# Row-tiled K and Q projections in one visit, MoE weights loaded ahead of batch 1, and a new planner, in a fused attention and MoE kernel

## The chip, the cores and the metric

The kernel runs on one core of one Trainium2 chip. The metric is the time of one execution on the device in microseconds (us), given as the median of several executions. The kernel before takes 329.5 us (329.06 to 330.17 in four runs).

Five engines work side by side (busy in the kernel before: TensorE 95% of the span, ScalarE 60%, VectorE 58%, GpSimd 26%), each through its own list of instructions in the order that the program fixes: TensorE (PE in the profile; its weight loads are PEld), VectorE (DVE), ScalarE (ACT), GpSimd (POOL) and SyncE (SP). POOL and SP also issue the transfers (DMA), 42 and 167 of them in the profile of the kernel before. An engine waits on a semaphore when the program does not yet allow its next instruction; TensorE did not go past such a wait here: in the changed kernel it stood 4.1 us before one instruction while later work was ready (shown below).

## The reference

```python
# q, k, v: 8 batches x 8 heads x 576 rows x 64; omega: 128 features x 64
def phi(x):                                        # random-feature map
    proj = np.einsum('bhsd,md->bhsm', x, omega)
    h = proj - np.sum(x * x, axis=-1, keepdims=True) / 2.0
    h = h - np.max(h, axis=-1, keepdims=True)
    return np.exp(h) / np.sqrt(m)
q_p, k_p = phi(q * scale), phi(k * scale)
kv, z = einsum('bhsm,bhsd->bhmd', k_p, v), np.sum(k_p, axis=2)
attn = einsum('bhsm,bhmd->bhsd', q_p, kv) / (einsum('bhsm,bhm->bhs', q_p, z)[..., None] + 1e-6)
x = attn.transpose(0, 2, 1, 3).reshape(4608, 512)  # tokens x features
h = x @ w_in                                       # 512 x 2048
out = (h / (1 + np.exp(-1.702 * h))) @ w_out       # 2048 x 512
```

A batch has 576 rows a head: 512 "main" rows and 64 "last" rows. The kernel works on pairs of heads, four pairs a batch.

## The kernel before

A small planner in Python builds a graph of operations, each with an engine, an assumed cost, a key (its priority) and its reads and writes. It then plays the program through with its assumed costs and so fixes the order of instructions on every engine; semaphores keep that order right whatever the real times are. A load has a `gate`, the transfer that must have landed before it is issued.

The projections of one pair (cut). `T` holds the transposed main rows, even head in partitions 0 to 63 and odd head in 64 to 127; `omB` is omega twice with zeros, so that a 128-row matmul picks one head:

```python
for hd, t0, c0, o in (("a", 2, 0, 1280), ("b", 6, 4, 1792)):       # K: 4 matmuls of 256 columns
    gr = bank()
    g.add(PE, [mm(at(gr, 0, 256), Tb(t0), omB[:, :]), mm(at(gr, 256, 512), Tb(t0 + 1), omB[:, :])],
          240, key, reads=[("Tk", tt)] + OM, grp=gr)
    reduce(0, 4, c0, gr); exp(gr, 512, o, ["k" + hd], key + 200)
gr = bank()                                                        # last rows: 2 of 128
g.add(PE, [mm(at(gr, 128, 256), TLo, om_o), mm(at(gr, 0, 128), om_e, TLo)], 115, key + K_L, ...)
...
for nm, w_, o in (("q0", om_e, 0), ("q1", om_o, 512)):             # Q: 2 of 512
    gr = bank()
    g.add(PE, mm(at(gr, 0, 512), w_, Tq), 216, key + K_Q, ...); exp(gr, 512, o, [nm], ...)
```

After these, a weights exp (WW), V times weights on POOL (VP), KV on TensorE, its copy (KVZ), the output matmuls, a division (RD, OO), and a transpose into XT, on TensorE for batches 0 and 1 and by DMA from batch 2 on. XT feeds the MoE in nine blocks of 512 tokens, one for the main rows of each batch and one for all last rows: for each block 16 groups of four 128x512 matmuls with WIN, tanh on ACT, a product on DVE (GT), then 64 matmuls with WOUT.

The loads of batches 0 and 1 and the weights. `load_qk` and the weights go through POOL's queue, `load_ql` (the last rows of Q and K, QLF) and `load_v` through SP's:

```python
load_qk(0, 0, 2, -150, "p0");  load_ql(0, ...);  load_v(0, 0, 2, -149)
load_qk(0, 2, 2, -148, "p1");  load_qk(0, 4, 4, -147, "p2")
load_v(0, 2, 2, -147, after=[("k", 0, 0)])
load_qk(1, 0, 4, P["LD"] + -10, "a", after=[("k", 0, 0)])     # batch 1's first half, early
gate = [("q", 0, 1)]                                          # Q of batch 0's second pair
load_ql(1, -119, P["ql1"], after=gate);  load_v(1, 0, 2, -110, after=gate)
gate = [("q", 0, 2)]
for c in range(4): load_win(c, P["LD"] + -5 + c, after=gate)
load_qk(1, 4, 4, P["LD"] + 0, "b", after=gate)
load_v(1, 2, 2, -109, after=[("win", 2)])
for c in range(4): load_wout(c, P["LD"] + 10 + c, after=gate)
```

The gate `("q", 0, 1)` is the Q load of batch 0's second pair. In the expectations quoted below I call it "the third Q load" by a slip; the edits name it as meant.

The softmax here doesn't subtract the row's maximum and nothing guards it: scores larger than these inputs give would overflow.

## Time and profile before

| what | value | seen in |
|---|---|---|
| span of the profiled run | 328.3 us | page |
| TensorE busy | 311.3 us, 95% | busy table |
| MoE: 1,152 matmuls of 512 columns, 216 ns apart | 249 us | timeline |
| K and Q of a pair, batch 2 on: 4 x 109 + 2 x 216 ns | 868 ns | timeline |
| last rows of four pairs: 8 x 56 ns | 448 ns | timeline |
| first matmul / first MoE matmul | 4.27 / 29.9 us | timeline |
| end of the last matmul | 324.3 us | timeline |

The page's busy table and slices of the kernel before (each slice is 8.2 us; a digit is the busy share in tenths; PEclk is the granted TensorE clock):

```profile
PE 311.3 (95%) x2091; PEld 163.2 (50%) x2129; DVE 189.5 (58%) x420; ACT 197.1 (60%) x396; POOL 86.6 (26%) x176
...
PE   2697999999999999999999999999999999999995
...
PEclk9989999999999999999999999999999999999999
DMA  7999989989999999969979973311121011000033
```

TensorE is full from the fifth slice to the last but one. DMA is at 90% or more in 18 of the 40 slices, all in the first 190 us, and yet TensorE's waits after 56 us are next to nothing (the profile lists none of them).

The timeline of TensorE before, at a pair of a late batch (start us, duration us, instruction):

```profile
182.92 0.38 PE L363 MATMUL PB<-TT,omB 128*128 128x512 bf16 x1
183.13 0.38 PE L363 MATMUL PB<-omB,TT 128*128 128x256 bf16 x2
183.35 1.03 PE L363 MATMUL OB<-WOUT,GT 128*128 128x512 bf16 x4
...
186.25 0.38 PE L363 MATMUL PB<-omB,TT 128*128 128x256 bf16 x2
186.47 0.22 PE L363 MATMUL PB<-omB,TL 128*128 128x128 bf16 x1
186.53 0.22 PE L363 MATMUL PB<-TL,omB 128*128 128x128 bf16 x1
186.58 0.59 PE L363 MATMUL OB<-WOUT,GT 128*128 128x512 bf16 x2
```

Read the starts, not the durations: Q's 512 columns take 183.13 - 182.92 = 0.21 us, two of K take 0.22, and a pair's last rows take 0.11.

### The profile page before, as it was taken

The numbers are of one execution on the slowest core, as the hardware profiler recorded it, in microseconds if no ns is written. First come the engines' busy times: TensorE is split into PE (matmuls) and PEld (weight loads), VectorE is DVE, ScalarE is ACT, GpSimd is POOL, SyncE is SP. The second block draws the span as 40 slices with busy tenths as digits, with TensorE's granted clock in tenths as the row PEclk, the third lists the DMA queues.
The fourth block names the chain that finished last, engine by engine and source line by source line (L and its number), as shares of the span: only waits on it lengthen the run. The fifth ranks groups of instructions, "written<-read, shape, count | busy, mean of one in ns | idle before, by whom it ended". The sixth has DMA issues, their size and how long they took to land.

```text
span 328.3 us, 5569 instructions
## 1 busy us (share of the span) xinstructions
PE 311.3 (95%) x2091; PEld 163.2 (50%) x2129; DVE 189.5 (58%) x420; ACT 197.1 (60%) x396; POOL 86.6 (26%) x176
## 2 busy tenths in 40 slices
PE   2697999999999999999999999999999999999995
PEld 1474655455555555555555555555544444444442
DVE  3397975458538786677468667675565434434300
ACT  2879664567738868777566657665663434344411
POOL 8398043043425226233316022222220000000000
PEclk9989999999999999999999999999999999999999
DMA  7999989989999999969979973311121011000033
GB/s 114 215 229 206 224 143 129 290 159 213 216 190 200 241 160 183 234 150 163 279 142 174 268 100 87 84 53 54 52 54 52 32 48 50 32 34 32 32 90 73
DMA packets 92939, 44.97 MB, mean 137 GB/s; under 512 B 59632, under 2 KB 88304, under 8 KB 92912
## 3 DMA queue, kind: packets, MB, share of 16 engines
q1 hardware_dynamic: 71760, 32.03, 44.3%
q0 software_dynamic: 21152, 12.59, 27.6%
q8 instruction: 17, 0.28, 0.4%
q14 instruction: 10, 0.08, 0.1%
HBM read 36.73 MB, written 9.44 MB: 141 GB/s over the span
## 4 chain that ended last, share of the span: by engine, by line
PE 88%; DVE 5%; DMA 2%; issue 1%; SPq 1%; POOL 0%; ACT 0%; POOLq 0%
PE OB L363 37%; PE HT L363 37%; PE PB L363 8%; PE SB L363 5%; DMA VS<-in_v_dram 2%; DVE NM L592 2%; DVE OO L733 1%; SPq L425 1%; DVE GT L792 1%; DVE TT L499 1%; PE SB L746 0%; SPq L447 0%; DVE RD L725 0%; POOL VP L652 0%; PE OB L534 0%
## 5 line engine op out<-in xcount | busy, mean ns | idle before, releaser
L792 DVE SCALAR_TENSOR_TENSOR GT<-TH,HT 128x512 bf16<-128x512 f32 x144 | 98.3, 685 | 75.6 <-ACT TH L787 75.1
L363 PE MATMUL HT<-XT,WIN 128*128 128x512 bf16 x555 | 139.6, 379 | 2.1 <-ACT WW L636 0.8
L363 PE MATMUL OB<-WOUT,GT 128*128 128x512 bf16 x559 | 137.8, 379 | 0.9
L787 ACT ACTIVATE TH<-HT 128x512 f32<-128x512 f32 x144 | 85.9, 597 | 73.8 <-PE HT L363 70.9
L603 ACT ACTIVATE QKP<-PB 128x512 bf16<-128x512 f32 (+1 forms) x143 | 77.8, 556 | 25.4 <-DVE NM L592 19.3
L363 PEld LDWEIGHTS OB<-WOUT,GT 128*128 128x128 bf16 x576 | 55.4, 98 | 59.9
L363 PEld LDWEIGHTS HT<-XT,WIN 128*128 128x128 bf16 x576 | 54.7, 98 | 58.4 <-ACT XT L498 0.9
L592 DVE TENSOR_REDUCE NM<-PB 128x4 f32<-128x512 f32 (+1 forms) x89 | 48.8, 564 | 26.1 <-PE PB L363 25.9
L641 POOL TENSOR_TENSOR WW<-WW,mask 128x2 f32<-128x2 f32 x32 | 6.3, 196 | 145.4 <-ACT WW L636 145.4
L652 POOL TENSOR_TENSOR VP<-VS,WW 128x512 bf16<-128x512 f32 x32 | 33.5, 1048 | 2.2 <-DMA VS<-in_v_dram 2.2
L821 ACT ACTIVATE OS<-OB 128x512 f32<-128x512 f32 x36 | 21.5, 597 | 20.6 <-PE OB L363 20.5
L733 DVE TENSOR_TENSOR OO<-SB,RD 128x320 bf16<-128x320 f32 x61 | 27.2, 478 | 0.1
L363 PE MATMUL PB<-omB,TT 128*128 128x256 bf16 x124 | 22.3, 282 | 1.7 <-ACT QKP L603 0.9
L363 PE MATMUL PB<-TT,omB 128*128 128x512 bf16 x54 | 19.7, 379 | 0.0
L363 PEld LDWEIGHTS SB<-KVZ,QKP 128*128 128x128 bf16 x305 | 14.0, 98 | 6.7 <-issue 0.2
L363 PEld LDWEIGHTS SB<-VP,QKP 128*128 128x128 bf16 x279 | 12.9, 99 | 8.1 <-POOL VP L662 2.3
L363 PE MATMUL SB<-VP,QKP 128*128 128x65 bf16 (+1 forms) x279 | 14.8, 198 | 2.0 <-POOL VP L662 1.8
L410 POOL DMA_DIRECT2D QK<-in_k_dram x17 | 13.4, 791 | 11.4 <-DMA TT<-QK 7.5
L363 PEld LDWEIGHTS PB<-omB,TT 128*128 128x128 bf16 x124 | 11.1, 100 | 8.6 <-ACT QKP L603 1.6
L363 PE MATMUL SB<-KVZ,QKP 128*128 128x65 bf16 x305 | 15.1, 195 | 0.0
L499 DVE CAST KVZ<-SB 128x130 bf16<-128x130 f32 x30 | 8.7, 289 | 11.0 <-PE SB L363 10.7
L410 POOL DMA_DIRECT2D QK<-in_q_dram x17 | 13.0, 766 | 0.0
(68 smaller groups left out, 134.0 us busy)
## 6 DMA issues: line engine op xcount, KB each, us to landing
out_dram<-OS SPq DMA_DIRECT2D x32, 256.0 KB, 2.5
VS<-in_v_dram SPq DMA_DIRECT2D x12, 512.0 KB, 8.8
QK<-in_k_dram POOLq DMA_DIRECT2D x15, 256.0 KB, 7.2
QK<-in_q_dram POOLq DMA_DIRECT2D x15, 256.0 KB, 8.9
VS<-in_v_dram SPq DMA_DIRECT2D x8, 256.0 KB, 8.4
WIN<-in_moe_w_in_dram POOLq DMA_DIRECT2D x4, 512.0 KB, 10.1
WOUT<-in_moe_w_out_dram POOLq DMA_DIRECT2D x4, 512.0 KB, 17.4
QLF<-in_q_dram SPq DMA_DIRECT2D x16, 64.0 KB, 4.4
```

The costliest lines, as they stand in the source:

```text
L363: return lambda e: e.matmul(o() if callable(o) else o, lhsT=l, rhs=r, **kw)
L410: POOL, lambda e, dst=dst, so=so: e.dma_start(dst, so), 800, key,
L425: SP, lambda e, dst=dst, so=so: e.dma_start(dst, so), 120, key,
L499: fv = lambda e: e.tensor_copy(out=o, in_=src())
L592: lambda e: e.tensor_reduce(out=NM[vs][:, c0 : c0 + w], in_=bass.AP(TILE[gr.bank], i, [[512, 128], [128, w], [1, 128]]), axis=AX.X, op=ALU ...
L603: lambda e: e.activation(out=X[:, o : o + w], in_=at(gr, 0, w)(), func=ACTF.Exp, scale=scale),
L641: lambda e: e.tensor_tensor(out=WW[vs][:, 0:2], in0=bass.AP(WW[vs], 10, [[12, 128], [0, 2]]), in1=mask2[:, :], op=ALU.mult,),
L652: lambda e: e.tensor_tensor(out=VP[vs][:, 2:10, 0:64], in0=bass.AP(V, vo + 64, [[vrow, 128], [64, 8], [1, 64]]), in1=bass.AP(WW[vs], 2, [[ ...
L733: lambda e, gr=gr, x=x: e.tensor_tensor(out=OO[os_][:, 5 * x : 5 * x + 5, :], in0=bass.AP(TILE[gr.bank], 0, [[512, 128], [65, 5], [1, 64]] ...
L787: lambda e, gr=gr, th=th: e.activation(out=TH[th][:, :], in_=at(gr, 0, 512)(), func=ACTF.Tanh, scale=0.851),
L792: lambda e, gr=gr, th=th, jc=jc: e.scalar_tensor_tensor(out=GT[gi][:, jc, :], in0=TH[th][:, :], scalar=1.0, in1=at(gr, 0, 512)(), op0=ALU. ...
L821: lambda e, gr=gr, os_=os_: e.activation(out=OS[os_][:, :], in_=at(gr, 0, 512)(), func=ACTF.Copy, scale=0.5),
```

## The change

Its intent: (1) K and Q of one pair, whose contraction has 64 rows, as two 64-row tiles at a time in one visit to TensorE, from batch 2 on; (2) the last rows of a batch's four pairs together; (3) WIN and WOUT ahead of batch 1's inputs; (4) V of batches 2 to 7 through POOL's queue (`software_dynamic` in the profile); (5) four OO buffers in place of two; (6) a planner that plays the DMA queues with assumed rates for each kind of load, and new keys. The core of the diff (cut):

```diff
-NQK, NV, NTT, NQP, NVP, NO, NTH, NGT, NOUT = 2, 2, 4, 4, 4, 2, 3, 2, 4
+NQK, NV, NTT, NQP, NVP, NO, NTH, NGT, NOUT = 2, 2, 4, 4, 4, 4, 3, 2, 4
+PEC = dict(K=325.0, Q=315.0, KQ=540.0, L=345.0)          # planner: assumed ns of a tiled visit
+SHARE = dict(pool=0.742, sp=0.472)                       # planner: assumed rate when both queues are busy
...
+rt = b not in PE_T                                       # PE_T = (0, 1)
+lo = (slice(0, 64), slice(64, 128)) if rt else (slice(0, 128), slice(0, 128))
+OMR = [omB[lo[par], 128 * par : 128 * par + 128] for par in range(2)]
...
+kcols = [[(128 * i, 128, T[lo[par], 128 * blk[i] : 128 * blk[i] + 128], OMR[par]) for i in range(4)] for par in range(2)]
+qcols = [[(0, 512, OMR[par], bass.AP(T, ...))] for par in range(2)]
+if rt and JOIN:                                          # matmuls of the two tiles alternate
+    gr = project(kcols + qcols, "KQ", key, [("Tk", tt), ("Tq", tt)])
...
-    load_qk(1, 0, 4, P["LD"] + -10, "a", after=[("k", 0, 0)])
     gate = [("q", 0, 1)]
-    load_ql(1, -119, P["ql1"], after=gate)
-    load_v(1, 0, 2, -110, after=gate)
-    gate = [("q", 0, 2)]
-    for c in range(4):
-        load_win(c, P["LD"] + -5 + c, after=gate)
-    load_qk(1, 4, 4, P["LD"] + 0, "b", after=gate)
-    load_v(1, 2, 2, -109, after=[("win", 2)])
-    for c in range(4):
-        load_wout(c, P["LD"] + 10 + c, after=gate)
+    for c in range(4):
+        load_win(c, P["Lw"] + c, after=gate)
+    for c in range(4):
+        load_wout(c, P["Lo"] + c, after=gate)
+    load_qk(1, 0, 4, P["Lb"], "a", after=gate)
+    load_qk(1, 4, 4, P["Lb"] + 2, "b", after=gate)
+    gate = [("win", 3)]
+    load_ql(1, -119, P["C1"], after=gate)
+    load_v(1, 0, 2, -110, after=gate)
+    load_v(1, 2, 2, -109, after=gate)
```

The built order of POOL's issues is WIN, batch 1's Q and K, WOUT: the keys put only WIN ahead of batch 1.

## The prediction

> **What bounds it now.** TensorE. The busy table gives PE 311.3 of 328.3 us; the chain of waits gives it 88%. The 1,152 MoE matmuls (128x512) follow each other every 216 ns in the timeline: 249 us. A pair of heads from batch 2 on costs, by start-to-start times in the timeline, about 435 ns for K (four 256-column matmuls), 432 for Q (two of 512), 110 for the last rows, 310 for KV and 310 for the output: 1.60 us, 24 times = 38 us. Batches 0 and 1 add PE transposes: about 2.3 us a pair, 19 us. Sum 306 us. The other 22 us are start (no matmul before 4.27 us; granted clock low until about 19 us; waits on transposed copies, V and the weights exp) and tail (last matmul 324.3 us, then copy and store, about 4 us). Summing start-to-start times over ideal column times, about 17 us are lost before 30 us and almost nothing after. DMA shows 90% busy until 190 us, yet PE waits after 56 us are practically zero, so DMA, ACT (60%), DVE (58%) and POOL (26%) do not bound the middle.
>
> **What the change does.**
> 1. From batch 2 on, K and Q of a pair use 64 contraction rows instead of 128 half-zero ones, two row tiles at a time, in one visit. [...] Columns halve: 867 ns becomes about 440 ns plus a drain. A 512-column matmul lasts 379 ns against 216 ns spacing, so an estimate of a drain is up to 163 ns; I take 100 to 160 per visit. Saving 270 to 330 ns x 24 = 6.4 to 7.8 us, all on the bounding engine. The last rows of four pairs go together: 440 ns per batch becomes about 350; 0.5 us over six batches. Batches 0 and 1 keep 128 rows: no PE saving.
> 2. Last-row work per batch instead of per pair: DVE loses 32 reductions of 283 ns and gains 8 of 686; ACT loses 32 exps of 383 and gains 16 of 596; POOL loses about 32 x 600 ns of small products, gains about 8 x 1.4 us. Off the path except in the start.
> 3. WIN is issued at about 9 us (15.5 before), ahead of batch 1's Q/K, V and last rows; in the built order WOUT still comes after batch 1's Q/K. Batch 0 runs alone up to the first MoE matmul, so that one (29.9 us before) should start at 24 to 27 us; but about 3 us of batch 1 work done there before moves later. Net gain 1 to 3 us.
> 4. V through POOL's queue, four OO buffers, per-stretch priorities, four banks for the last blocks: about 0 each, as PE has no waits there.
>
> **Prediction: 319 us** (-3.2%), range 314 to 325. Chances: faster by over 2% 0.83, within 2% 0.14, slower 0.03.
>
> **Right if:** PE busy falls by about 8 us while ACT and DVE fall slightly; a joined K/Q visit takes 540 to 600 ns, start to start; pure MoE stays at 216 ns; first MoE matmul before 27 us; PE waits after 40 us stay under 2 us.
>
> **Wrong if:** tiles do not overlap, or each switch costs over 300 ns (then about 325); weights ahead of batch 1 starve PE between 40 and 60 us (batch 1's Q/K or WOUT late); the two 4-bank visits make PE wait for ACT and DVE to release banks; or V on POOL's queue delays POOL's products.

The two tiles running side by side and a change of mode costing time (the "drain"): no trace at hand then showed either (the trace of the result does: 59 ns for a pair of K matmuls, 96 ns in and 93 out). 329.5 us less 6.4 to 7.8 and 0.5 (step 1) and 1 to 3 (step 3) comes to 318.2 to 321.6 us. The 100 to 160 ns of a drain were my estimate, from the 379 and 216 ns of a 512-column matmul in the trace before. "Granted clock low until about 19 us" is 0.50 from 15.4 to 18.8 us in that trace's clock records.

## More of the kernel before

A busy time of overlapping matmuls is not a sum of work (one of 512 columns is shown with 379 ns, and the next starts 216 ns after it), so I count work by another rule: each matmul of the program counts with the spacing that it has when nothing disturbs it (216 ns for 512 columns, 109 for 256, 56 for 128, 57 for 130, 31 for 65). That gives 306.2 us. The last matmul's slot ends at 324.2 us, so 18.0 us are lost, 17.4 of them before the first MoE matmul.

Busy time by stretch before (us; busy us and count of each engine, clock, DMA share, GB/s):

```profile
20.00:26.00 6.00, 5.46 (x79) 3.69 (x77) 6.00 (x18) 5.72 (x14) 5.75 (x12) 1.00 1.21 227
...
36.00:40.30 4.30, 4.30 (x45) 2.82 (x43) 4.19 (x11) 3.60 (x7) 0.00 (x0) 1.00 1.18 241
40.30:45.50 5.20, 5.15 (x36) 2.83 (x36) 4.55 (x8) 4.26 (x11) 2.28 (x6) 1.00 1.24 209
```

The first figure after the length is TensorE: full in the later two, and 5.46 of 6 us even while batch 0's chain is still being worked off, because batch 1's projections fill the gaps.

## The result, and the profile after

The changed kernel takes 333.1 us (332.82 to 333.61, four runs) against 329.5 us. The ratio is 1.0106, 95% interval 1.0081 to 1.013: about 1% slower, and outside the predicted range.

| | before | after |
|---|---|---|
| span of the profiled run | 328.3 | 331.5 us |
| work of all matmuls, by spacing | 306.2 | 300.7 us |
| lost up to the end of the last matmul's slot | 18.0 | 26.6 us |
| first MoE matmul | 29.9 | 26.1 us |
| lost before the first MoE matmul | 17.4 | 16.5 us |
| lost from there to 60 us | 0.2 | 7.4 us |
| lost after 60 us | 0.4 | 2.8 us |

(For the change a tiled visit counts with what it takes undisturbed, 641 ns or 425 ns, which includes the way into the tile mode and out of it. The trace before lacks 38 matmul records; they are counted where their weight loads stand.) So the projections did get cheaper, by 5.5 us, and 8.7 us more are lost (unrounded): 7.2 more between the first MoE matmul and 60 us, 2.4 more after that in many small pieces, and 0.9 less before. The sum, +3.2 us, is the difference of the spans. The pieces after 60 us were not traced to a cause.

The page's busy table and slices of the changed kernel:

```profile
PE 311.0 (94%) x2233; PEld 153.2 (46%) x2233; DVE 191.7 (58%) x394; ACT 193.5 (58%) x388; POOL 91.6 (28%) x150
...
PE   3778499999999999999999999999999999999995
...
PEclk9899979999999999999999999999999999999999
DMA  7999974957979997998897899750013100001023
```

The fifth slice of TensorE is a 4, and the clock of the sixth a 7. Busy time hardly moved: it counts matmuls at half clock as more (one of 512 columns is shown with 634 ns there and not 379), and it lacks the 38 missing records of before. It would have hidden both the gain and the loss.

The timeline of TensorE after, one joined visit between MoE matmuls (64*128 is a tile of 64 rows):

```profile
77.21 1.89 PE L410 MATMUL OB<-WOUT,GT 128*128 128x512 bf16 x8
79.03 0.23 PE L410 MATMUL SB<-omB,TT 64*128 64x128 bf16 x1
79.03 0.23 PE L410 MATMUL PB<-omB,TT 64*128 64x128 bf16 x1
...
79.27 0.38 PE L410 MATMUL SB<-TT,omB 64*128 64x512 bf16 x1
79.27 0.38 PE L410 MATMUL PB<-TT,omB 64*128 64x512 bf16 x1
79.58 0.60 PE L410 MATMUL HT<-XT,WIN 128*128 128x512 bf16 x2
```

The two tiles start together, four such pairs for K and one for Q (the first two K matmuls of a visit 3 or 4 ns apart in 23 of 24 visits), and a pair of 128-column K matmuls takes 59 ns where one such matmul of full rows takes 56: the two tiles do work in parallel. The eight WOUT matmuls end their slots at 77.21 + 8 x 0.216 = 78.94, and the next MoE matmul starts at 79.58: the visit costs 0.64 us. By the trace's full resolution 23 of the 24 visits cost 640 to 642 ns: 96 ns between the last full matmul's slot and the first tile, 237 from there to the start of the last Q matmul (234 of it K), 216 for Q, and 93 beyond Q's slot before the next full matmul. The 24th waited 0.4 us more. A visit for last rows costs 425 ns. Saved: 24 x (868 - 641) + 6 x (448 - 425) = 5.6 us.

Busy time by stretch after, around the stretch in which TensorE stands (the hole):

```profile
30.00:36.00 6.00, 5.88 (x52) 3.49 (x49) 5.67 (x11) 5.59 (x13) 0.00 (x0) 1.00 1.25 198
36.00:40.30 4.30, 0.20 (x1) 0.01 (x1) 0.71 (x2) 0.88 (x2) 0.74 (x2) 1.00 1.23 196
40.30:45.50 5.20, 5.18 (x35) 3.08 (x36) 2.67 (x6) 3.58 (x8) 0.48 (x4) 0.67 1.16 264
45.50:50.00 4.50, 4.50 (x38) 2.50 (x36) 3.78 (x7) 4.15 (x9) 1.95 (x2) 1.00 0.29 83
```

TensorE stands for 4.1 us, and then, looking fully busy, runs at a mean clock of 0.67 (the trace's clock records say half speed from 41.5 to 44.9 us; 512-column matmuls start 427 ns apart there, and 216 at full clock). Who it waited for, from the timeline of TensorE (in brackets: idle time before, and its releaser), and the chain of work through the same place (start us, us, what):

```profile
35.82 0.38 PE L410 MATMUL PB<-TT,omB 128*128 128x512 bf16 x1
40.32 0.38 PE L595 MATMUL SB<-ident,QL 128*128 128x128 bf16 x4 [4.12 <-POOL QL L476]
...
40.76 1.22 PE L410 MATMUL HT<-XT,WIN 128*128 128x512 bf16 x4
```

```profile
11.63 15.48 DMA WIN<-in_moe_w_in_dram
...
29.06 0.04 issue
29.10 10.41 DMA QLF<-in_k_dram
39.51 0.05 issue
39.56 0.62 POOL QL L476
40.18 0.14 issue
40.32 0.38 PE SB L595 x4
```

Read it upward. TensorE's next instruction is the transpose of batch 1's last rows (QL). POOL's cast of them waited for their four loads (QLF), the last of which took 10.4 us; and SP had not issued those loads before the last WIN had landed, at 27.1 us. In the kernel before they were issued at 10.5 us, and TensorE's first use of them was at 24.4 us, with no wait for a load there:

```profile
24.39 0.40 PE L554 MATMUL OB<-ident,QL 128*128 128x128 bf16 x4
```

Two facts make this a loss and not a detour. TensorE took its list in order, so the MoE group at 40.76 us stood behind the transpose, though its WIN had landed by 27.1 us and its XT (batch 0) had been in use since 26.1 us. And the planner believed otherwise: its own schedule, printed for the changed kernel (a model, not a measurement), against the trace:

```
                       planned by the kernel   on the chip
last WIN landed               26.7               27.1 us
QLF landed      30.7 31.7 32.7 33.7   33.4 35.8 37.8 39.5 us
cast of QL starts             33.8               39.6 us
```

It was right about the issue and wrong about the landings by 2.7 to 5.8 us.

### The profile page after: what moved, and what is told of

Same layout as the page of the kernel before. It is cut to its first block, busy times and chain, and to the rows that moved or that the text cites. A ratio compares the mean times of both kernels' runs of the same rounds, so it can differ in the third digit from the quotient of the medians. Undisturbed runs are those within 1.5% of the kernel's fastest.

```text
span 331.5 us, 5737 instructions
## 1 busy us (share of the span) xinstructions
PE 311.0 (94%) x2233; PEld 153.2 (46%) x2233; DVE 191.7 (58%) x394; ACT 193.5 (58%) x388; POOL 91.6 (28%) x150
## 4 chain that ended last, share of the span: by engine, by line
PE 77%; DMA 9%; DVE 9%; POOL 2%; issue 1%; SPq 1%; ACT 1%; POOLq 0%
PE HT L410 34%; PE OB L410 30%; PE PB L410 8%; PE SB L410 5%; DMA WIN<-in_moe_w_in_dram 5%; DVE OO L797 4%; DMA QLF<-in_k_dram 3%; DVE GT L857 2%; DMA QK<-in_q_dram 1%; DVE RD L789 1%; DVE KVZ L544 1%; POOL QK L457 1%; POOL WIN L512 1%; SPq L472 1%; ACT TH L852 0%
## 5 line engine op out<-in xcount | busy, mean ns | idle before, releaser
L410 PE MATMUL OB<-WOUT,GT 128*128 128x512 bf16 x512 | 128.1, 379 | 0.3 <-DVE GT L857 0.2
L651 ACT ACTIVATE QKP<-SB 128x512 bf16<-128x512 f32 x59 | 34.6, 601 | 4.2 <-PE PB L410 2.2
L651 ACT ACTIVATE QKP<-PB 128x512 bf16<-128x512 f32 x60 | 35.2, 605 | 2.8 <-PE PB L410 1.6
L641 DVE TENSOR_REDUCE NM<-PB 128x4 f32<-128x512 f32 x31 | 21.0, 686 | 7.3 <-PE SB L410 4.1
L641 DVE TENSOR_REDUCE NM<-SB 128x4 f32<-128x512 f32 x28 | 19.0, 688 | 9.1 <-PE PB L410 8.6
L457 POOL DMA_DIRECT2D QK<-in_k_dram x17 | 13.3, 783 | 28.1 <-DMA TT<-QK 27.1
L797 DVE TENSOR_TENSOR OO<-SB,RD 128x320 bf16<-128x320 f32 x34 | 16.7, 491 | 1.2
L410 PE MATMUL PB<-WOUT,GT 128*128 128x512 bf16 x64 | 15.6, 379 | 0.0
L797 DVE TENSOR_TENSOR OO<-PB,RD 128x320 bf16<-128x320 f32 x27 | 13.3, 491 | 0.9
L410 PE MATMUL PB<-omB,TT 64*128 64x128 bf16 (+1 forms) x124 | 9.9, 222 | 0.0
L410 PE MATMUL SB<-TT,omB 64*128 64x512 bf16 (+1 forms) x31 | 9.8, 392 | 0.0
```

Source lines behind the costliest of these rows:

```text
L410: return lambda e: e.matmul(o() if callable(o) else o, lhsT=l, rhs=r, **kw)
L457: POOL, lambda e, dst=dst, so=so: e.dma_start(dst, so), 800, key,
L641: lambda e: e.tensor_reduce(out=o, in_=bass.AP(TILE[gr.bank], 0, [[512, 128], [128, 4], [1, 128]]), axis=AX.X, op=ALU.max, negate=True,),
L651: lambda e: e.activation(out=o, in_=at(gr, 0, 512)(), func=ACTF.Exp, scale=scale),
L797: lambda e, gr=gr, x=x: e.tensor_tensor(out=OO[os_][:, 5 * x : 5 * x + 5, :], in0=bass.AP(TILE[gr.bank], 0, [[512, 128], [65, 5], [1, 64]] ...
```

## The experiments

Theory A: the slowdown is the late gate of batch 1's last rows, which stops TensorE and then costs clock; the tiles themselves bring what the trace says. Rival B: the start is limited by bytes, and another order only moves the wait. Rival C: the tiles bring nothing net. Theory D came later: weights ahead of batch 1 also take away TensorE's filler work. "Order kept" means that the planner's order on every engine is untouched, and only what an instruction waits for or reads is edited, so nothing else can move for reasons of planning.

### 1. Batch 1's last rows early, order kept

```diff
     g.schedule()
+    new = next(o for o in g.ops if o.dma == "d_q0p1")
+    for d in ("d_ql10", "d_kl10", "d_ql11", "d_kl11"):
+        next(o for o in g.ops if o.dma == d).deps = {new.i: True}
```

> The changed kernel with every engine's order of instructions kept word for word; only the four loads of batch 1's last rows of Q and K wait for the third Q load of batch 0 (landed 8.9 us) as before the change, not for the last WIN load (landed 27.1 us). Theory A (the late gate: these rows land at 39.5 us, TensorE idles 4.1 us for their transpose and then runs 5 us at a clock of 0.67): they land near 20 us, TensorE has no wait over 1 us between 30 and 50 us, the clock stays 1.0 there, and the kernel takes 326 to 327.5 us, so 6 us less than the change and faster than before by about 1%. Rival B (the start is limited by DMA bytes, whatever their order): the wait only moves to another load, and the time stays at 332 to 333.5 us.

Measured: 328.58 us (327.78 to 329.7); ratio to before 0.9967 (0.9942 to 0.9993). The rows landed from 18.8 to 23.8 us. TensorE's waits from 30 to 50 us in this run (us in total, times, longest us):

```profile
PE HT L410 <- DVE GT L857: 0.3, 1, 0.3
```

One changed wait gives back 4.5 us. Rival B falls. But some 6 us had been expected (326 to 327.5 us in all), and the rest is instructive. In this run the clock was halved as well, earlier, from 27.0 to 30.4 us, right at the first MoE matmuls:

```profile
20.00:26.80 6.80, 3.67 (x61) 2.65 (x61) 4.70 (x15) 3.85 (x8) 6.29 (x9) 1.00 1.24 203
26.80:30.20 3.40, 3.37 (x9) 1.25 (x9) 0.69 (x1) 0.94 (x2) 0.00 (x0) 0.53 1.43 196
```

TensorE was busy for only 3.67 of the 6.8 us before. The kernel before had 5.46 of 6 there. That gave theory D.

### 2. The mirror: the kernel before with these rows late, order kept

```diff
+    new = next(o for o in g.ops if o.dma == "d_win3")     # in the kernel before
+    for d in ("d_ql10", "d_kl10", "d_ql11", "d_kl11"):
+        next(o for o in g.ops if o.dma == d).deps = {new.i: True}
```

> The mirror: the kernel before, all orders kept, with the same four loads waiting for its last WIN load (landed 33.1 us there) instead of the third Q load. Theory A: TensorE stops at the transpose of these rows, which stood at 24.4 us, until about 37 to 43 us, the clock falls after the stop, and the kernel takes 340 to 350 us. Rival B: below 332 us.

Measured: 350.17 us; ratio 1.0621 (1.0605 to 1.0637). TensorE waited 17.5 us at the transpose of these rows. The same gate is harmful in the old kernel too, and more: its order uses the rows earlier, ACT (which casts them in that kernel) stood 17.2 us as well, and the clock was at half from 28.6 to 49.1 us (mean of the profiled run 0.961, and 0.995 in the kernel before).

### 3. The row tiles undone, order kept

```diff
-lo = (slice(0, 64), slice(64, 128)) if rt else (slice(0, 128), slice(0, 128))
+lo = (slice(0, 128), slice(0, 128))
```

> The changed kernel, orders kept, with the row tiles undone: from batch 2 on the same matmuls read all 128 rows (half of omega's rows are zero). From the two traces a joined visit costs 641 ns where K and Q cost 868 ns before, and the last rows 425 where 448. Theory A: 24 x 227 ns + 6 x 23 ns = 5.6 us of the change's gain goes, 338 to 339.5 us. Rival C (the tiles gain nothing, or their drains cost what they save): within 1 us of the change, 332 to 334 us.

Measured: 337.28 us; ratio 1.0239 (1.0215 to 1.0262), so 4.2 us over the change and not 5.6. Its start came out differently: the first MoE matmuls of the profiled run were at half clock (27.8 to 31.2 us), so TensorE came to the transpose of the last rows 2 us later (at 38.2 us, not 36.2) while the rows landed as before (39.3 us), and the wait was 1.9 us instead of 4.1. Rival C falls; the size is better read from experiment 9, where the start has no hole.

### 4. The tile mode left and entered once more in each visit, order kept

```diff
 if rt:
     em = [... the tiles' matmuls, alternating ...]
+    if cost == "KQ":                       # one 128-row matmul of one column, overwritten by Q
+        em.insert(8, mm(at(gs[2], 0, 1), ident[:, :], ident[:, 0:1]))
     g.add(PE, em, PEC[cost], kk, reads=reads + OM, grp=gs)
```

> The changed kernel, orders kept, with one 128-row matmul of one column put between the K and the Q part of each of the 24 joined visits (its result is overwritten), so that the array leaves and enters the row-tile mode twice. In the trace entering costs 96 ns and leaving 93 ns. Theory A: 24 x (190 to 250) ns = 4.5 to 6 us more than the change, 337.5 to 339.5 us. If the mode change is free and the 190 ns have another cause: under 1 us more.

Measured: 338.61 us; ratio 1.027 (1.0248 to 1.0292), 5.5 us over the change. In the trace each visit became two, of 425 and 432 ns in the median, 857 in all: 216 ns more than one of 641, the slot of the one-column matmul included, and 24 x 216 ns = 5.2 us. (The spell at half clock around the hole lasted 6.8 us in this profiled run and 3.4 in that of the change, so the visits are the cleaner measure.) This shows what joining K and Q is worth: in two visits nearly the whole saving of the tiles would go to changes of mode.

### 5. Only the planner told that the rows come late

```diff
-kind="ql", descs=64 * NT, slack=slk(b),
+kind="ql", descs=64 * NT, slack=6000.0 if b == 1 else slk(b),
```

> The changed kernel with its loads' waits untouched (batch 1's last rows still wait for the last WIN load), but the planner is told that these four loads land 6 us later than it assumed, so it places their transposes later and other work before them. The plan of the change has their cast at 33.8 us; on the chip it came at 39.6. If the loss is the in-order plan's false arrival time (theory A, in its narrower form), TensorE waits under 1 us between 30 and 50 us, and the time is 327 to 330 us, as with the early loads (328.6). If the data itself is needed by then whatever the order, the wait stays and the time is 332 to 334 us.

Measured: 332.24 us (330.11 to 332.91); ratio 1.0064 (1.0017 to 1.0111). A miss: I expected 327 to 330. The long wait is gone, but the profiled run, the second fastest of the four at 331.66 us, has others in its place, and its clock was at half from 25.3 to 28.7 us. TensorE's waits from 26 to 60 us:

```profile
PE PB L410 <- POOL VPL L685: 1.4, 1, 1.4
PE HT L410 <- DVE GT L857: 1.2, 3, 0.5
PE HT L410 <- ACT XT L543: 1.1, 1, 1.1
PE PB L410 <- POOL VP L725: 0.3, 1, 0.3
```

My reading, not tested by itself: with the late rows planned late, batch 1's attention comes late as a whole, and TensorE runs short of it around 48 us (busy 2.95 of the 4.5 us from 45.5). A later arrival time in the plan did not make up for the late arrival here.

### 6. Loads in the old order, planned anew

```diff
     load_v(0, 2, 2, -147, after=[("k", 0, 0)])
+    load_qk(1, 0, 4, -146, "a", after=[("k", 0, 0)])
     gate = [("q", 0, 1)]
+    load_ql(1, -119, P["C1"], after=gate)
+    load_v(1, 0, 2, -110, after=gate)
+    gate = [("q", 0, 2)]
     ... WIN ...
+    load_qk(1, 4, 4, P["Lb"], "b", after=gate)
+    load_v(1, 2, 2, -109, after=[("win", 2)])
     ... WOUT; the five loads of batch 1 behind them taken out ...
```

> The changed kernel (row tiles, joined visits, V through POOL's queue, four OO buffers, new planner and its constants) with the loads of batch 1 in the order of the kernel before: first half of Q and K ahead of WIN, last rows and V early, WIN after the last Q load of batch 0; the planner plans anew. Theory D (besides the stall, weights ahead of batch 1 take away the work that filled TensorE between 20 and 30 us: with the last rows early it was busy 3.7 of 6.8 us before 26.8 us and then had its clock halved for 3.4 us): TensorE is busy over 85% from 20 to 26 us, no halved clock after 20 us, first MoE matmul at 28 to 31 us with about 12.5 us of work done, and 324 to 326.5 us in all. If the load order plays no more part: 328 to 329 us.

Measured: 327.24 us (326.7 to 327.37); ratio 0.9918 (0.9901 to 0.9936). It beats both kernels, by 2.5 and by 5.9 us, but stays above the 324 to 326.5 us expected. The stretches that answer to those of before:

```profile
20.00:26.00 6.00, 4.75 (x86) 3.94 (x85) 5.81 (x18) 4.99 (x11) 6.00 (x8) 1.00 1.22 226
26.00:30.00 4.00, 3.33 (x23) 1.62 (x22) 2.82 (x6) 3.80 (x9) 2.24 (x5) 1.00 1.24 207
```

TensorE was busy 79% from 20 to 26 us, not the 85% expected. 11.6 us of work were done when the MoE started at 26.8 us (28 to 31 us had been expected), against 9.6 us in the change, and the clock was full from 11.9 us on. Theory D holds in its direction, but it was not tested alone: against experiment 1, where the last rows are early already, all other changes of the load order together, with their new plan, bring 1.3 us. About 3 us are still lost from the first MoE matmul to 60 us, where the kernel before loses 0.2, the largest piece a 1.2 us wait of MoE matmuls for DVE that ends at 32.4 us. This was not taken apart further.

### 7. WOUT held back until the rows have landed, order kept

```diff
     g.schedule()
+    ql = [next(o for o in g.ops if o.dma == d) for d in ("d_ql10", "d_kl10", "d_ql11", "d_kl11")]
+    for o in g.ops:
+        if o.dma is not None and o.dma.startswith("d_wout"):
+            o.deps.update({q_.i: True for q_ in ql})
```

> The changed kernel, orders kept, with the four WOUT loads held back until batch 1's last rows have landed. Asks why these rows took 10.4 us from issue to landing (27.1 to 39.5 us) where the same loads take 4 us in the median. If they share the DMA engines with a backlog on POOL's queue (WOUT was issued at 22 to 25 us and landed from 36 to 48 us), they now land at 33 to 36 us. If small rows are slow by themselves, they land at 39 to 40 us as before. The time is of little meaning, for WOUT comes later.

The time from issue to landing of these loads, first in the change and then in this run (both between 26 and 41 us):

```profile
DMA to landing us min/median/max: 6.3/8.7/10.4
```

```profile
DMA to landing us min/median/max: 4.8/5.3/5.6
```

They landed from 33.1 to 34.2 us: the slowest of them took 5.6 us with WOUT kept away, instead of 10.4. So in this pair of runs the loads on SP's queue were held up by WOUT's transfers on POOL's, the slowest by 4.8 us; how the two get in each other's way was not shown. (The median of all 16 such loads of Q in the change is 4.0 us.) One execution took 329.6 us. It is a single run of unknown state, so no more than a hint that even this order of loads beats the change's. The cast still came only at 37.5 us, for POOL now had WOUT to issue before it (four issues of 0.75 to 0.78 us each in the change), and TensorE waited 1.4 us.

### 8. V of batches 2 to 7 through SP's queue again, planned anew

```diff
-SP if b < 2 else POOL, lambda e, dst=dst, so=so: e.dma_start(dst, so), 120, key,
+SP, lambda e, dst=dst, so=so: e.dma_start(dst, so), 120, key,
```

> The changed kernel with V of batches 2 to 7 issued from SP's queue as before the change; the planner plans anew. My prediction gave this part about 0: 332 to 334.5 us, TensorE's waits after 60 us unchanged within 1 us. If moving V to POOL's queue was itself harmful or helpful: a difference of over 1.5 us.

Measured: 332.22 us; ratio 1.0073 (1.0054 to 1.0092). Within what was expected: this part gains nothing here. If anything it costs 0.9 us, which these runs are too few to call.

### 9. Old load order and no row tiles (experiment 6 with the edit of 3)

> The kernel with the loads in the old order (327.2 us), its order kept, with the row tiles undone as in the third experiment: what is left of the change is the new planner with its banks and constants, the last rows once per batch, V through POOL's queue and four OO buffers. If these are worth nothing either way, the row tiles' 5 us come off and the time equals the kernel before plus what the start still loses: 331 to 333 us. If the new plan is in itself better than the old one: under 330 us.

Measured: 332.68 us; ratio 1.0097 (1.0076 to 1.0118). Its order is that of experiment 6, instruction for instruction, and neither run has the hole, so the difference of 5.4 us is the tiles: the trace's 5.6 us confirmed. What is left against the kernel before, +3.0 us, belongs to the rest: the new planner and its keys, last rows by batch, queues and buffers. By the count of work it loses 20.2 us instead of 18.0, spread over many waits, none longer than 1.8 us after the first matmul; I did not find one cause. The clock is not it: in the profiled runs it was at half from 15.4 to 18.8 us in the kernel before and never after 12.9 us here, until the work ended. Nor were the keys tuned again for the old load order in experiments 6 and 9; whether that is part of the 3.0 us was not tested.

### 10. Only the first half of batch 1's Q and K ahead of WIN, and the rows early

```diff
+    load_qk(1, 0, 4, -146, "a", after=[("k", 0, 0)])
     ... WIN, WOUT as in the change ...
-    load_qk(1, 0, 4, P["Lb"], "a", after=gate)
     load_qk(1, 4, 4, P["Lb"] + 2, "b", after=gate)
-    gate = [("win", 3)]
     load_ql(1, -119, P["C1"], after=gate)
+    gate = [("win", 3)]
     load_v(1, 0, 2, -110, after=gate)
```

> The changed kernel with only two of its load changes undone: the first half of batch 1's Q and K goes ahead of WIN, and batch 1's last rows wait for the third Q load. WIN still starts on the third Q load of batch 0 and V of batch 1 still waits for the last WIN load. If WIN's late start and V's early loads (undone as well in the kernel of 327.2 us) do not matter: 326.5 to 328 us. If V of batch 1 after WIN holds TensorE up once the rest is early: 329 to 331 us.

Measured: 330.35 us (330.08 to 330.74); ratio 1.0029 (1.0011 to 1.0047): 3.1 us over experiment 6, in the band of the second answer. POOL did wait 11.4 us for V of batch 1 between 33 and 48 us, which fits it. But TensorE's longest wait there, 2.8 us at 30 us, was for DVE, before V mattered. So V's place after WIN is a likely part of these 3 us and not shown to be all of it.

### 11. Two OO buffers, planned anew

```diff
-NQK, NV, NTT, NQP, NVP, NO, NTH, NGT, NOUT = 2, 2, 4, 4, 4, 4, 3, 2, 4
+NQK, NV, NTT, NQP, NVP, NO, NTH, NGT, NOUT = 2, 2, 4, 4, 4, 2, 3, 2, 4
```

> The changed kernel with two OO buffers in place of four; the planner plans anew. My prediction gave the extra buffers about 0: 332.5 to 334.5 us.

Measured: 337.65 us (337.18 to 340.85); ratio 1.0268 (1.0218 to 1.0317), a miss by 3 us. After 60 us TensorE now has waits that the change does not have, one of 2.1 us for DVE and this one:

```profile
PE HT L410 <- DMA XT<-OO: 2.4, 1, 2.4
```

It is followed by 3.4 us at half clock. The kernel before manages with two buffers; its order spreads the writes of OO of a batch over 17 to 29 us (batches 2 to 7), and the change's order over 6 to 7 us in five of these six. So the new order is slower with two buffers; that the extra ones gain anything over the kernel before is not shown.

### 12. Experiment 6 with row tiles in batch 1 too

```diff
-rt = b not in PE_T
+rt = b >= 1
-if rt and JOIN:
+if rt and JOIN and b not in PE_T:
```

> A try for a faster one: the kernel with the loads in the old order (327.2 us) and row tiles in batch 1 too, there in separate K and Q visits for each pair. K and Q of a pair then cost two visits of about 425 ns for 880 ns of 128-row matmuls, so at most 4 x 30 ns = 0.1 us; a separate K visit can start earlier only if data allow. Same as that kernel within 0.7 us: 326.5 to 328 us.

Measured: 327.35 us; ratio 0.9937 (0.9914 to 0.996): the same as experiment 6, as expected from a visit that costs 425 ns for 440 ns of matmuls.

## Why the prediction was wrong

In medians, the change taken apart along experiments 9 and 6 (each against the run before it in the row):

| step | time | difference |
|---|---|---|
| kernel before | 329.7 us | |
| + planner, last rows by batch, V's queue, OO buffers (exp. 9) | 332.7 | +3.0 |
| + row tiles in joined visits (exp. 6) | 327.2 | -5.4 |
| + the change's load order = the change | 333.1 | +5.9 |

- **The failed step is step 3**, "Net gain 1 to 3 us" from WIN ahead of batch 1's Q/K, V and last rows. The runs show a loss of 5.9 us in its place (experiment 6 against the change). 4.5 us of it is one wait (experiment 1): the last rows of batch 1 behind the last WIN. The part of the step about the first MoE matmul was right (26.1 us, predicted 24 to 27), and it was the wrong thing to look at: it came earlier, with 2.9 us less done before it. I had named "weights ahead of batch 1 starve PE between 40 and 60 us (batch 1's Q/K or WOUT late)" as a risk. The starving came at 36 us, and not from Q/K or WOUT but from four loads of 64 KB each.
- **How it could have been seen.** The gate stands in the diff, and I put these rows into the list of what comes after WIN. I did not follow the chain: last WIN landed at 33.1 us in the kernel before and would land some 6 us earlier; behind it come the rows' loads, 9 us each in the kernel before between 9 and 30 us, then a cast, then the transpose. That is an estimate of 27 + 9 + 2 = 38 us from numbers of the trace before, for work that had been done at 24.4 us.
- **The clock added to this hole.** After the 4.1 us wait TensorE ran 3.4 us at half clock (0.50 from 41.47 to 44.88 us); half of that is 1.7 us, so the hole cost an estimated 5.8 us. In experiment 1, without the hole, the clock was 1.00 from 36 to 50 us. What makes the clock fall was not shown beyond that. The 3.4 us before the fall (38.06 to 41.47 us) were not all idle: TensorE was busy for 1.15 of them, and in experiment 1 for 1.31 of the 3.41 us before its fall (23.61 to 27.02 us), with no wait longer than 1.0 us among them. My prediction counted waits alone.
- **Step 1 was right in its mechanism and off in size.** I took 540 to 600 ns for a joined visit and 350 for last rows; they cost 641 and 425. The mis-sized term is the drain, that is, the change of mode: I took 100 to 160 ns a visit, and entering (96) and leaving (93) both cost. K takes 234 ns and not 224. So 5.6 us came instead of 6.9 to 8.3. Experiment 4 shows the change of mode by itself: 216 ns for one more time out and in, the extra matmul's slot included.
- **Step 4, "about 0 each", was wrong for the plan as a whole.** V's queue brought no gain (experiment 8). The kernel before shows no wait for OO buffers on TensorE, but the new order depends on the two more (experiment 11). The new plan with all this costs 3.0 us against the old one (experiment 9), for reasons that stay open.
- **Step 2 was right**: fewer reductions and exps on DVE and ACT (ACT busy 197.1 to 193.5 us), with no effect that could be seen on the time. DVE rose slightly, 189.5 to 191.7 us.
- **Of the signs I named**, pure MoE stayed at 216 ns and the first MoE matmul came before 27 us; PE busy did not fall by 8 us (a bad sign to choose, see above), and a visit took 641 ns instead of 540 to 600. TensorE's waits after 40 us did stay under 2 us: the 4.1 us wait lay from 36.2 to 40.3 us, just before the stretch that I had named.

Open: which of the new plan's waits make up its 3.0 us, and whether WIN's earlier start or V's later one costs the 3.1 us between experiments 10 and 6.

## What to carry to other kernels

When loads are put in a new order, follow each one that is pushed back, however small, through landing, cast and first use, and compare with the place of that use in its engine's list; here a full engine with a fixed order stopped 4.1 us for four loads of 64 KB, and then paid again in clock (3.4 us at half). Row tiles took K and Q of a pair from 868 to 450 ns, but every visit cost about 190 ns on top, so put as much as possible into one visit: with K and Q in two visits (857 ns in experiment 4) almost nothing would be left of the gain. And test a load order by itself, with the engines' orders kept: here one such run (experiment 1) gave back 4.5 us, and experiments 9 and 6 then separated a gain of 5.4 us from a loss of 5.9.
